# Cached attention on one core: V in products of N 512, kept K in pairs of N 256, shorter chain bursts, and wo in runs of 1792 B

## The chip, the core and the metric

The kernel runs on one core of a Trainium2 chip. The metric is the device time of one execution in microseconds (us), and a kernel's number is the median of its runs. Executions of one kernel on one chip spread by about 0.4% either way here (1114.97 to 1125.07 us in one set of the changed kernel), so a difference of 3 us or less between two kernels is mostly not resolved. All timed runs quoted below were in the fast state, except the single run of experiment 10, whose state can't be told.

## The reference, cut to what matters

Two passes, each of attention over a cache and of a small MLP block, for eight batch rows with one query token each. There are 16 query heads on 8 K/V heads of width 256, and 4096 cached keys. Everything is bf16, and D is 448.

```python
x = x + _A_ref(_layernorm(x), A_k_cache, A_v_cache, A_wq, A_wo)   # attention
x = x + _B_ref(_layernorm(x), B_w1, B_w2, B_w3, B_w4)             # MLP block
x = x + _A_ref(_layernorm(x), A_k_cache, A_v_cache, A_wq, A_wo)   # the same caches again
x = x + _B_ref(_layernorm(x), B_w1, B_w2, B_w3, B_w4)

# _A_ref: scores = q k^T / 16, p = softmax(scores), o = p v, then o.reshape(B, 1, 4096) @ wo
```

K and V are 134 MB each. Pass 2 of a row needs the result of pass 1 of that row, and the same K and V again. What the kernel can't keep in SBUF in between it has to read twice.

## The kernel before

K and V come in chunks of 1 MB. SBUF has 15 "places" of one chunk each. While a batch row goes from its first pass to its second, 11 of its chunks stay in their places (the kept ones), and so only 4 places are left for everything else to stream through. A place is given back when its chunk has been used, and the next load into it is issued at once:

```python
NC = 15
kept = [(GP - 1, kv, n) for n in range(4) for kv in range(2)] + [(GP - 2, 0, n) for n in range(3)]
slots = [consts.tile([128, 16 * Dh], BF16, name=f"slot{n}") for n in range(NC)]
...
for idx, it in enumerate(items):            # one item = one chunk of K (kv 0) or V (kv 1)
    ...
    if kv == 0:
        transpose_k(slot)                   # two DVE stream transposes, 1.2 us each
        step(idx)                           # the chain may put one burst here
        scores(slot, c, st["q"], gp)        # 32 products, N 128
        if c == 0 and n - 1 in p_of:
            transpose_p(p_of.pop(n - 1))    # p of the task before: 4 products and an ACT cast
        ...
    else:
        step(idx)                           # and here
        pv(st["o", g8], slot, c, gp, begin=...)   # 16 products, N 256
        ...
    if not (ps == 0 and stays(it)):
        places.append(p)
    emit_loads()                            # loads into the places that are free
    step(idx)                               # and here
```

The "chain" is what turns one row's o into the q of its second pass: normalisation, wo, layer norms, the MLP and wq. It is a Python generator. Each `yield` ends one burst of it, and `step` places the next burst between the chunks, in the program order of the engines:

```python
def add_cols(y_ps, rhs, w, rows, every, open=None):
    for fc in range(5):
        ...
        for i in rows:
            nc.tensor.matmul(r, w[:, i, lo:hi], rhs(i), ...)
        ...                                 # a yield after every `every` columns fc

def half(o_ps, zall, g8, OT):               # evacuation of o: twice per row and pass
    rz = yield from z_cols(zall, range(2 * g8, 2 * g8 + 2))
    R = chn.tile([128, 8], FP32, tag="R")
    ...
    nc.scalar.copy(o_sb[:], o_ps[:, 0:Dh])
    in_use.remove(o_ps)
    yield
    for j in range(2):
        nc.tensor.matmul(ot_ps[:, j], o_sb[:, 128 * j : 128 * j + 128], R[:], start=True, stop=True)
    yield
    nc.vector.tensor_copy(OT[:, :, 8 * g8 : 8 * g8 + 8], ot_ps)
    yield
```

Each engine's instructions stand in one program order, and the dip shown below has them run in it: a V product waits there behind a burst of the chain although its data has landed. A burst that stands ahead of the scores or of V can delay these, with them the moment at which the place is free, and with that the next load.

The softmax here doesn't subtract the row's maximum and nothing guards it: scores larger than these inputs give would overflow.

Of the kernel before, what the change touches and what calls it, by code (L numbers as in the profile page):

```python
# [8 lines left out]
FP32 = mybir.dt.float32  # L9
# [8 lines left out]
def kernel(  # L18
# [52 lines left out]

    slots = [consts.tile([128, 16 * Dh], BF16, name=f"slot{n}") for n in range(NC)]

# [21 lines left out]
    for u in range(2):  # L95
# [6 lines left out]

    fold = consts.tile([128, 8], FP32, name="fold")
    nc.vector.tensor_reduce(
        fold[:],
        ident.rearrange("p (q n) -> p n q", q=4)[:, 0:8],
        mybir.AxisListType.X,
# [169 lines left out]
    def project_q(b0, nb, qT):  # L277

        yield from norm(xT[:, :, b0 : b0 + nb], nb, False)
        q_ps = room_ps("q", nb).rearrange("p (c b) -> p c b", b=nb)  # L280
        for j in range(2):
            for h in range(Hq):
                for fc in range(4):
                    w, xi = wblk(wq_sb, HD, 2 * h + j, fc)
                    nc.tensor.matmul(  # L285
                        q_ps[:, j * Hq + h, :],
                        w,
                        xbs(nb)[:, xi, :],
                        start=(fc == 0),
                        stop=(fc == 3),  # L290
                    )
                if h % 8 == 7:
                    yield
        nc.vector.tensor_copy(qT, q_ps)
        yield
# [54 lines left out]
    def mlp_hidden(b0, nb):  # L350
# [3 lines left out]
        for c in range(HC):  # L354
            for fc in range(4):
                w, xi = wblk(w3_sb, F, c, fc)
                nc.tensor.matmul(  # L357
                    h_ps[:, c * nb : c * nb + nb],
                    w,
                    xbs(nb)[:, xi, :],  # L360
                    start=(fc == 0),
                    stop=(fc == 3),
                )
            if c == HC // 2:
                yield
# [25 lines left out]
    def mlp(b0, nb):  # L391
        HT = yield from mlp_hidden(b0, nb)
        yield from out_cols(lambda c: HT[:, c, :], w4_sb, HC, b0, nb, 2)

# [31 lines left out]
    def half(o_ps, zall, g8, OT):  # L426


        rz = yield from z_cols(zall, range(2 * g8, 2 * g8 + 2))

        R = chn.tile([128, 8], FP32, tag="R")
        nc.vector.tensor_mul(
            R[:].rearrange("p (g n) -> p g n", n=4),
            rz[:].rearrange("p n g -> p g n"),
            fold[:].rearrange("p (g n) -> p g n", n=4),
        )
        o_sb = chn.tile([128, Dh], FP32, tag="o_sb")
        nc.scalar.copy(o_sb[:], o_ps[:, 0:Dh])  # L438
        in_use.remove(o_ps)
        yield  # L440
        ot_ps = ot_bank[:, 32 * g8 : 32 * g8 + 16].rearrange("p (j h) -> p j h", j=2)
        for j in range(2):
            nc.tensor.matmul(  # L443
                ot_ps[:, j], o_sb[:, 128 * j : 128 * j + 128], R[:], start=True, stop=True
            )
        yield
        nc.vector.tensor_copy(OT[:, :, 8 * g8 : 8 * g8 + 8], ot_ps)
        yield
# [3 lines left out]
    def first_half(b, st):  # L452

        OT = work.tile([128, 2, Hq, 1], BF16, tag="OT", bufs=1)
        st["OT"] = OT
        yield from half(st["o", 0], st["z"], 0, OT[:, :, :, 0])
        yield from add_cols(
            y_room(1)[:, 0], lambda i: OT[:, i % 2, i // 2], wo_sb, range(NB2 // 2), 2
        )

    def chain(b, st):
        OT = st["OT"]
        yield from half(st["o", 1], st["z"], 1, OT[:, :, :, 0])
        yield from add_cols(
            y_room(1)[:, 1], lambda i: OT[:, i % 2, i // 2], wo_sb, range(NB2 // 2, NB2), 2
        )
# [90 lines left out]
    where = {}  # L557

    def emit_loads(most=None):
        n = 0  # L560
        while loads and places and n != most:
            it = loads.pop(0)
            p = where[it] = places.pop(0)
            if stays(it):
# [20 lines left out]

    def scores(t, x, qbd, gp):
        kv = t[:].rearrange("p (k t e i r) -> p k e r t i", k=4, t=4, e=4, r=2)
        for n in range(8):
            half, e2, par = n // 4, (n // 2) % 2, n % 2
            ep = 4 * e2 + 2 * par + half  # L590
            for k in range(4):
                nc.tensor.matmul(  # L592
                    sc[32 * k : 32 * k + 8, 128 * x : 128 * x + 128],
                    qbd[:, ep, gp].rearrange("p a h -> p (a h)"),
                    kv[:, k, 2 * half + e2, par],
                    start=(n == 0),
                    stop=(n == 7),
                )
# [41 lines left out]
    def pv(o_ps, v, a, gp, begin):  # L640


        g = 2 * gp + a // 2
        for y in range(16):
            q = y % 4
            at = 128 * a + 8 * (4 * q + y // 4) + 6 - 2 * (g % 4)
            nc.tensor.matmul(  # L647
                o_ps[32 * q : 32 * q + 8, 0:256],
                ptz[:, at : at + 8],
                v[:, y * Dh : (y + 1) * Dh],  # L650
                start=(begin and y < 4),
                stop=(y >= 12),
                skip_group_check=True,
            )

    def pv_cols(o_ps, v, a, gp):

        g = 2 * gp + a // 2
        for y in range(16):
            for j in range(2):  # L660
                nc.tensor.matmul(  # L661
                    o_ps[:, j, 2 * g : 2 * g + 2],
                    v[:, y * Dh + 128 * j : y * Dh + 128 * j + 128],
                    ptw[:, a, 4 * (y % 4) + y // 4, 6:8],
# [12 lines left out]
    emit_loads(5)  # L677
    nc.sync.dma_start(wo_sb[:], A_wo.rearrange("(g p) d -> p g d", p=128))
    load_split(w3_sb, B_w3, F)
# [16 lines left out]
    def step(idx):  # L696

        for kind in ("chain", "last", "rest"):
# [5 lines left out]
            if e["n"] < e["of"] * (idx - e["at"] + 1) / max(e["until"] - e["at"], 1):  # L704
                e["n"] += 1
                if next(e["g"], gens) is gens:
                    gens.remove(e)

    first_of = {}
    for idx, (n, kv, c) in enumerate(items):  # L710
# [3 lines left out]
    for idx, it in enumerate(items):  # L714
        n, kv, c = it
        ps, b, gp = tasks[n]
        if (ps, b, gp, kv, c) == (0, Bn - 1, REST, 0, 0):
            assert pairs_done[1, MID - 1] == 4
            add_gen("rest", 0, rest(), idx + 1, idx + 18, 21)
        p = where[(b, gp), (kv, c)] if ps == 1 and (stays(it) or inside(it)) else where[it]  # L720
        slot = slots[p]
        final = (ps, b) == (1, Bn - 1)
        if kv == 0:
# [19 lines left out]
            step(idx)  # L743
            scores(slot, c, st["q"], gp)
            if c == 0 and n - 1 in p_of:
                transpose_p(p_of.pop(n - 1))
            if c == 1:
# [7 lines left out]
        else:  # L755
# [34 lines left out]
            if c == 3:  # L790
                done = pairs_done[ps, b] = pairs_done.get((ps, b), 0) + 1
                if done == 2 and ps == 0:
                    add_gen("chain", b, first_half(b, st), idx + 1, idx + 21, 9)
                elif done == 2:
                    add_gen("chain" if final else "last", b, first_last(b, st), idx + 1, idx + 13, 9)
                elif done == 4 and ps == 0:
                    add_gen("chain", b, chain(b, st), idx + 1, first_of[(1, b), 0] - 1, 30)
                elif done == 4 and not final:
                    add_gen("last", b, last(b, st), idx + 1, idx + (7 if b == Bn - 2 else 13), 6)
        if not (ps == 0 and stays(it)):  # L800
# [78 lines left out]
```

## Time and profile before

| | before |
|---|---|
| time, median (lowest to highest) | 1128.83 us (1124.52 to 1134.04), 6 runs |
| span of the profiled execution | 1124.9 us |
| TensorE busy | 63% |
| bytes moved by the core's queue | 446.80 MB |
| lack against 420 GB/s, worked out from the row of GB/s: first two slices / middle / last slice | 7.8 / 30.9 / 16.6 us |

The last row is the way in which this document counts. The page has 40 equal slices with the GB/s of each. What a slice lacks to 420, times the length of a slice, divided by 420, is the time for which the stream stood still; slices above 420 count as no lack. The same sum is used for every kernel below.

The groups of instructions that the change touches, from the kernel before's page. The columns are line, engine (PE is TensorE, DVE is VectorE, ACT is ScalarE), operation, output<-input, shapes and count, then total busy us and mean ns of one, then the engine's idle us just before them with what ended most of it:

```profile
L592 PE MATMUL sc<-slot,qbd 128*8 128x128 bf16 x8192 | 277.3, 292 | 297.0 <-DVE slot L584 241.5
L647 PE MATMUL o<-slot,ptw 128*8 128x256 bf16 x3968 | 248.1, 398 | 58.4 <-DMA slot<-in_A_v_cache_dram 39.6
L443 PE MATMUL misc<-R,o_sb 128*128 128x8 f32 x124 | 30.4, 356 | 1.1 <-ACT o_sb L438 1.1
```

The first is the scores, the second V, the third the products of the evacuation. The scores wait for the DVE transposes of K, and V waits for its DMA: TensorE is not what they lack.

How a burst of the chain costs stream time is seen in a dip, from the timeline of the kernel before (start us, length us, engine, line, what, in brackets the idle time before it and what ended it; SPq is the queue that issues loads):

```profile
141.91 2.19 PE L339 MATMUL misc<-OT,wo_sb 128*128 128x1 bf16 x48
...
144.03 1.03 PE L647 MATMUL o<-slot,ptw 128*8 128x256 bf16 x16
144.14 0.16 DVE L468 TENSOR_TENSOR xT<-xT,misc 128x4 f32<-128x4 f32 x1 [2.81 <-PE misc L339]
...
145.00 2.36 DVE L584 STREAM_TRANSPOSE slot<-slot 128x1024 uint32<-128x1024 uint32 x2
145.10 0.33 SPq L576 DMA_DIRECT2D slot<-in_A_v_cache_dram  x1
...
148.06 0.33 SPq L576 DMA_DIRECT2D slot<-in_A_k_cache_dram  x1
```

By the semaphores of their loads, a V chunk had landed at 141.18 and a K chunk at 143.67. V waits on TensorE until the 48 products are through. Its place goes to the next load at 145.10, 3.91 us after the landing; a V chunk that nothing holds up takes 1.11 us (landed at 425.83). K waits on VectorE: the chain's additions and norms stand ahead of its transposes, and the first of them waited 2.81 us for the same burst. So the transposes start at 145.00, and the place goes at 148.06, 4.39 us after the landing instead of the usual 3.09. Not every burst costs this. The one at 387.33 that the prediction shows is as long, but it ran while the transposes of the next K did (from 387.42), and that K place was given back at 390.52, 3.10 us after they began. For the K before it that was 3.07 us (382.47 to 385.54).

The Trainium skill, "Perfetto Trace Analysis", Optimization Strategy, describes the pattern: the same gap, repeating for a stretch on what should be saturated, "can mean there isn't enough SBUF/PSUM for the next tile to be allocated". The trace agrees: the dips lie in the stretches with 4 free places, and a load that finds a place early, in a good stretch, takes 20 us from issue to landing, and one in a dip 7.8 us. That a further place would close the dips is not shown: the run that tried it (experiment 12) failed.

### The profile page before, as it was taken

The numbers are of one execution on the slowest core, as the hardware profiler recorded it, in microseconds if no ns is written. First come the engines' busy times: TensorE is split into PE (matmuls) and PEld (weight loads), VectorE is DVE, ScalarE is ACT, GpSimd is POOL, SyncE is SP. The second block draws the span as 40 slices with busy tenths as digits, with TensorE's granted clock in tenths as the row PEclk, the third lists the DMA queues.
The fourth block names the chain that finished last, engine by engine and source line by source line (L and its number), as shares of the span: only waits on it lengthen the run. The fifth ranks groups of instructions, "written<-read, shape, count | busy, mean of one in ns | idle before, by whom it ended". The sixth has DMA issues, their size and how long they took to land. (4 is left out here: it accounts for less than half of the span.)

```text
span 1124.9 us, 36977 instructions
## 1 busy us (share of the span) xinstructions
PE 707.0 (63%) x17173; PEld 518.8 (46%) x17173; DVE 590.0 (52%) x1009; ACT 123.9 (11%) x362; POOL 15.6 (1%) x25
## 2 busy tenths in 40 slices
PE   3145577556754577645784477745778477877776
PEld 2123456435642455424563255523556255655555
DVE  5145464646365555555465453655537553575462
ACT  0001001110110011100011001100111001111010
POOL 0000000000000000000000000000000000000000
PEclk9999999655575555555556555655555555565575
DMA  9999999999999999999999999999999999999994
GB/s 352 371 420 420 413 372 419 419 411 397 403 419 420 387 385 419 417 420 387 401 420 419 420 387 415 419 420 407 389 401 419 419 394 400 419 381 397 405 419 172
DMA packets 67241, 449.15 MB, mean 399 GB/s; under 512 B 6920, under 2 KB 12944, under 8 KB 13456
## 3 DMA queue, kind: packets, MB, share of 16 engines
q1 hardware_dynamic: 67056, 446.80, 98.0%
q8 instruction: 134, 2.20, 0.8%
q14 instruction: 19, 0.16, 0.0%
q10 hardware_dynamic: 32, 0.00, 0.0%
HBM read 446.77 MB, written 0.01 MB: 397 GB/s over the span
## 5 line engine op out<-in xcount | busy, mean ns | idle before, releaser
L584 DVE STREAM_TRANSPOSE slot<-slot 128x1024 uint32<-128x1024 uint32 x400 | 469.1, 1218 | 270.8 <-DMA slot<-in_A_k_cache_dram 270.5
L592 PE MATMUL sc<-slot,qbd 128*8 128x128 bf16 x8192 | 277.3, 292 | 297.0 <-DVE slot L584 241.5
L592 PEld LDWEIGHTS <-qbd 128*8 128x8 bf16 x8192 | 195.0, 108 | 374.3 <-issue 191.6
L647 PE MATMUL o<-slot,ptw 128*8 128x256 bf16 x3968 | 248.1, 398 | 58.4 <-DMA slot<-in_A_v_cache_dram 39.6
L601 ACT ACTIVATE p_n<-sc 128x256 bf16<-128x256 f32 x128 | 95.3, 745 | 769.9 <-PE sc L592 769.9
L647 PEld LDWEIGHTS <-ptw 128*8 128x8 bf16 x3968 | 111.8, 112 | 105.7 <-issue 54.3
L339 PEld LDWEIGHTS <-wo_sb 128*128 128x128 bf16 (+1 forms) x1600 | 62.6, 122 | 21.4 <-issue 20.8
L339 PE MATMUL misc<-OT,wo_sb 128*128 128x1 bf16 (+1 forms) x1280 | 53.5, 176 | 7.3 <-issue 5.2
L285 PEld LDWEIGHTS <-wq_sb 128*128 128x128 bf16 x1152 | 34.9, 104 | 24.6 <-issue 18.8
L311 DVE TENSOR_SCALAR qbd<-misc,quad 128x64 bf16<-128x64 f32 x64 | 13.7, 277 | 59.8 <-PE misc L305 59.8
L635 ACT CAST ptw<-misc 128x128 bf16<-128x128 f32 x64 | 17.4, 272 | 196.8 <-PE misc L628 105.6
L285 PE MATMUL misc<-xb,wq_sb 128*128 128x1 bf16 x1024 | 32.3, 166 | 7.9 <-DVE xb L260 4.4
L601 ACT ACTIVATION_READ_ACCUMULATOR p_n<-sc 128x1 f32 x128 | 34.0, 266 | 0.0
L443 PEld LDWEIGHTS misc<-R,o_sb 128*128 128x128 f32 x124 | 27.6, 310 | 10.2 <-issue 8.0
L443 PE MATMUL misc<-R,o_sb 128*128 128x8 f32 x124 | 30.4, 356 | 1.1 <-ACT o_sb L438 1.1
L243 POOL TENSOR_TENSOR t<-t,nhalf 128x2 f32<-128x2 f32 (+2 forms) x18 | 13.3, 739 | 1095.7 <-DVE t L250 1095.7
L339 PEld LDWEIGHTS <-w_sb 128*128 128x128 bf16 (+1 forms) x630 | 25.1, 125 | 7.3 <-issue 7.1
L357 PE MATMUL misc<-xb,w_sb 128*128 128x1 bf16 (+1 forms) x560 | 17.9, 166 | 12.4 <-DVE xb L260 7.4
L357 PEld LDWEIGHTS <-w_sb 128*128 128x128 bf16 x560 | 17.7, 105 | 17.0 <-issue 16.9
L412 PE MATMUL misc<-zm,one 128*128 128x8 f32 (+1 forms) x66 | 18.6, 352 | 9.8 <-ACT ptw L635 6.5
L619 DVE STREAM_TRANSPOSE slot<-store 128x512 uint32<-128x512 uint32 x32 | 20.1, 684 | 7.2 <-PE sc L592 7.2
L339 PE MATMUL misc<-HT_t,w_sb 128*128 128x1 bf16 (+1 forms) x560 | 22.8, 177 | 1.5 <-issue 1.2
(94 smaller groups left out, 239.5 us busy)
## 6 DMA issues: line engine op xcount, KB each, us to landing
slot<-in_A_v_cache_dram SPq DMA_DIRECT2D x216, 1024.0 KB, 11.6
slot<-in_A_k_cache_dram SPq DMA_DIRECT2D x200, 1024.0 KB, 12.1
wo_sb<-in_A_wo_dram SPq DMA_DIRECT2D x1, 3584.0 KB, 26.8
wq_sb<-in_A_wq_dram SPq DMA_DIRECT2D x3, 1024.0 KB, 7.0
w_sb<-in_B_w_dram SPq DMA_DIRECT2D x1, 1568.0 KB, 12.8
w_sb<-in_B_w_dram SPq DMA_DIRECT2D x3, 448.0 KB, 26.8
wq_sb<-in_A_wq_dram SPq DMA_DIRECT2D x2, 256.0 KB, 10.0
w_sb<-in_B_w_dram SPq DMA_DIRECT2D x2, 112.0 KB
```

The lines of the kernel that those rows point to most:

```text
L285: nc.tensor.matmul(q_ps[:, j * Hq + h, :], w, xbs(nb)[:, xi, :], start=(fc == 0), stop=(fc == 3),)
L311: nc.vector.tensor_scalar_mul(qbd[:, :, :, a, :], qs.rearrange("p e (f g u h) -> p (e f) u g h", f=2, u=2, h=2)[:, :, u], quad[:, a : a + 1],)
L339: nc.tensor.matmul(r, w[:, i, lo:hi], rhs(i), start=start, stop=stop, skip_group_check=open is not None,)
L357: nc.tensor.matmul(h_ps[:, c * nb : c * nb + nb], w, xbs(nb)[:, xi, :], start=(fc == 0), stop=(fc == 3),)
L412: nc.tensor.matmul(z_ps, ones, zm[:], start=True, stop=True)
L443: nc.tensor.matmul(ot_ps[:, j], o_sb[:, 128 * j : 128 * j + 128], R[:], start=True, stop=True)
L584: nc.vector.transpose(w, w)
L592: nc.tensor.matmul(sc[32 * k : 32 * k + 8, 128 * x : 128 * x + 128], qbd[:, ep, gp].rearrange("p a h -> p (a h)"), kv[:, k, 2 * half + e2, ...
L601: nc.scalar.activation(p_sb[:, :, :, 2 * u : 2 * u + 2].rearrange("p t i x -> p x t i"), sc[:, 256 * u : 256 * u + 256].rearrange("p (x t ...
L619: nc.vector.transpose(slot[:].bitcast(U32)[:, 512 * n : 512 * n + 512], store[n][:].bitcast(U32))
L635: nc.scalar.copy(ptw[:, :, :, 6:8], pt_ps.rearrange("p t k (a h) -> p a (t k) h", a=4),)
L647: nc.tensor.matmul(o_ps[32 * q : 32 * q + 8, 0:256], ptz[:, at : at + 8], v[:, y * Dh : (y + 1) * Dh], start=(begin and y < 4), stop=(y >= ...
```

## The change

The intent: fewer TensorE instructions for V and for kept K, no long bursts of the chain in front of the places' release, less work between a K chunk's landing and its release, and wo in longer DMA runs.

V takes two 256-wide blocks of a chunk per product (N of 512). The two land beside each other in o, with weights of 16 columns, so that o has two diagonal parts, and the evacuation needs two copies and twice the products:

```diff
-        for y in range(16):
-            q = y % 4
-            at = 128 * a + 8 * (4 * q + y // 4) + 6 - 2 * (g % 4)
-            nc.tensor.matmul(
-                o_ps[32 * q : 32 * q + 8, 0:256], ptz[:, at : at + 8],
-                v[:, y * Dh : (y + 1) * Dh], ...
+        rows = v[:].rearrange("p (i q d) -> p q i d", q=4, d=Dh)
+        for i in (0, 2):
+            for q in range(4):
+                at = 128 * a + 8 * (4 * q + i) + 6 - 2 * (g % 4)
+                nc.tensor.matmul(
+                    o_ps[32 * q : 32 * q + 16, :].rearrange("p (i d) -> p i d", i=2),
+                    ptz[:, at : at + 16], rows[:, q, i : i + 2], ...
...
-        nc.scalar.copy(o_sb[:], o_ps[:, 0:Dh])
+        for n in range(2):
+            nc.scalar.copy(o_sb[:], o_ps[:, Dh * n : Dh * n + Dh])
+            yield
+            for j in range(2):
+                nc.tensor.matmul(ot_ps[:, n, j], o_sb[:].rearrange("p (i j) -> p j i", j=2)[:, j], R[:, n], ...)
...
+        nc.vector.tensor_copy(half_o[:], ot_ps[:, 0])
+        nc.vector.tensor_add(to, half_o[:], ot_ps[:, 1])
```

The places become one tensor, loads choose neighbouring places for a pair of kept K chunks, and the pair is scored with one product of N 256 where they are neighbours. The transposition of p moves between the two halves of the scores:

```diff
-            scores(slot, c, st["q"], gp)
-            if c == 0 and n - 1 in p_of:
-                transpose_p(p_of.pop(n - 1))
+            turn = None
+            if c == TURN(n) and n - 1 in p_of:
+                turn = lambda t=p_of.pop(n - 1): transpose_p(t)
+            if not paired(n, c):
+                scores(p, c, st["q"], gp, between=turn)
+            elif c % 2 != ps:
+                ...
+                if abs(two[1] - two[0]) == 1:
+                    scores(two[0], x, st["q"], gp, also=two[1], between=turn)
```

The chain is cut into smaller bursts, and has more steps to be placed:

```diff
-                if h % 8 == 7:                 # wq
+                if h % 4 == 3:
-            if c == HC // 2:                   # w3
+            if c % 4 == 3:
-        yield from out_cols(lambda c: HT[:, c, :], w4_sb, HC, b0, nb, 2)
+        yield from out_cols(lambda c: HT[:, c, :], w4_sb, HC, b0, nb, 1)
-            y_room(1)[:, 0], ..., wo_sb, range(NB2 // 2), 2
+            y_room(1)[:, 0], ..., wo_sb, range(NB2 // 2), 1
-                    add_gen("chain", b, chain(b, st), idx + 1, first_of[(1, b), 0] - 1, 30)
+                    add_gen("chain", b, chain(b, st), idx + 1, first_of[(1, b), 0] - 1, 43)
```

Two neighbouring rows of wo lie on one partition, so that a run is 1792 B instead of 896 B. The last V chunks and the evacuation therefore take their weights with a column step of 2:

```diff
-    nc.sync.dma_start(wo_sb[:], A_wo.rearrange("(g p) d -> p g d", p=128))
+    nc.sync.dma_start(
+        wo_sb[:].rearrange("p (h j) d -> p h (j d)", j=2),
+        A_wo.rearrange("(h p j) d -> p h (j d)", p=128, j=2),
+    )
-                    v[:, y * Dh + 128 * j : y * Dh + 128 * j + 128],
+                    v[:, y * Dh + j : (y + 1) * Dh : 2],
```

## The prediction

> **What bounds the kernel now.** I read the head of the page first, then its row of GB/s, then the DMA issues and the engine shares of single stretches, and last the timeline of one slow stretch. Page, rows of the whole span and of its 40 slices:
>
> ```profile
> span 1124.9 us, 36977 instructions
> PE 707.0 (63%) x17173; PEld 518.8 (46%) x17173; DVE 590.0 (52%) x1009; ACT 123.9 (11%) x362; POOL 15.6 (1%) x25
> ...
> PEclk9999999655575555555556555655555555565575
> ...
> GB/s 352 371 420 420 413 372 419 419 411 397 403 419 420 387 385 419 417 420 387 401 420 419 420 387 415 419 420 407 389 401 419 419 394 400 419 381 397 405 419 172
> ```
>
> No compute engine is above 63%, while half of the slices move 417 to 420 GB/s, which is evidently what this stream can reach: 446.8 MB at 420 would need 1064 us. The kernel is a transfer with holes in it. A slice is 28.12 us; adding up what each lacks to 420 gives 826, and 826 x 28.12 / 420 = 55.3 us. Of it the first two slices hold 7.8 us (start, small packets), the last 16.6 us (work after the last transfer), and the rest 30.9 us, in eight dips that come every 100 to 135 us. What the change can win is in those 30.9 us and a little at the ends.
>
> What a dip is: stretches of 14.06 us (columns: length, busy of PE, PEld, DVE, ACT, POOL with counts, clock, DMA share, GB/s), two without a dip and three of one:
>
> ```profile
> 337.44:351.50 14.06, 6.54 (x148) 3.79 (x148) 8.78 (x10) 1.03 (x3) 0.00 (x0) 0.50 1.01 421
> 351.50:365.56 14.06, 6.34 (x148) 3.88 (x148) 7.11 (x6) 1.57 (x5) 0.00 (x0) 0.50 1.01 421
> 379.62:393.68 14.06, 10.85 (x224) 8.26 (x220) 6.78 (x16) 1.29 (x4) 0.00 (x0) 0.50 0.94 355
> 393.68:407.74 14.06, 9.10 (x232) 6.64 (x231) 9.18 (x21) 1.43 (x5) 0.70 (x1) 0.50 0.98 375
> 407.74:421.80 14.06, 11.41 (x259) 8.62 (x257) 6.72 (x17) 1.77 (x6) 0.55 (x1) 0.50 0.99 394
> ```
>
> The dips are where the "chain" (wo, norms, MLP, wq of one batch row) runs. They coincide with the phase in which 11 of the 15 places of SBUF hold kept chunks, so only 4 are left to stream through. The DMA issues of a dip (380 to 425 us) and of a good stretch (450 to 500 us), last column issue to landing:
>
> ```profile
> slot<-in_A_v_cache_dram SPq DMA_DIRECT2D x10, 1024.0 KB, 7.8
> slot<-in_A_k_cache_dram SPq DMA_DIRECT2D x8, 1024.0 KB, 7.9
> ...
> slot<-in_A_k_cache_dram SPq DMA_DIRECT2D x9, 1024.0 KB, 20.5
> slot<-in_A_v_cache_dram SPq DMA_DIRECT2D x8, 1024.0 KB, 20.2
> ```
>
> A landing of 20 us means eight transfers queued, 7.8 us two to three: in a dip the queue is short, because places come back late. A pair (one K and one V chunk) takes 5.0 us at 420 GB/s; the K transposes of this dip start at 377.79, 382.47, 387.42, 393.52, 398.47, 404.41, 409.46 and 415.21, that is 5.35 us apart. What PE and DVE do to a pair there, from the timeline:
>
> ```profile
> 377.79 2.36 DVE L584 STREAM_TRANSPOSE slot<-slot 128x1024 uint32<-128x1024 uint32 x2
> 379.08 0.60 PE L592 MATMUL sc<-slot,qbd 128*8 128x128 bf16 x16 [2.18 <-DVE slot L584]
> 380.20 0.60 PE L592 MATMUL sc<-slot,qbd 128*8 128x128 bf16 x16 [0.53 <-DVE zs_t L401]
> 381.95 1.02 PE L647 MATMUL o<-slot,ptw 128*8 128x256 bf16 x16
> 382.90 1.02 PE L443 MATMUL misc<-R,o_sb 128*128 128x8 f32 x4
> 387.33 2.19 PE L339 MATMUL misc<-OT,wo_sb 128*128 128x1 bf16 x48
> ```
>
> **What the Trainium skill says.** (1) "TensorE: Matmul & The Clock Gate", section Back-to-back issue gap: on the throttled clock products follow each other by N / 1.2 ns, so by columns streamed, not by instructions. The trace agrees: in the V burst at 381.95 the four column groups start within 12 ns of each other and the next four 213 ns later (256 / 1.2), and the clock column is 0.50 in nearly all slices after the first 200 us. The earlier 9s are not to be believed: score bursts there have the same 0.60 us. (2) The same page, Weight-path perf modes: fast weight load takes full 128-column weights with a column step other than 1. No record of the kernel before has such a step, so the trace is silent. (3) "DMA: Bandwidth & Descriptors", Why small descriptors are slow: a fixed cost per packet. The trace agrees: packets of 896 B take 47 ns, of 3584 B 145, of 8192 B 309.
>
> **The change part by part.**
>
> V in products of N 512: 3968 products become 1984. Columns streamed per group stay 4 x 256 = 2 x 512 = 1024, 853 ns at half clock. Only issue falls away, and it was not the limit, so a burst should stay about 1.0 us. Value in the dips: about 0.
>
> Kept K in pairs of N 256: reading the changed program, 56 pairs occur, and 35 lie in neighbouring places and so merge; 35 x 32 = 1120 products fewer of 8192. Again the same columns. And kept chunks are scored while filling or draining the places, where the DMA row stands at 419 to 421, not in the dips. Value 0. Choosing neighbours holds a load back 21 times, by one or two chunks, with 13 to 15 chunks still ahead: no cost. The order of the 416 loads is the same in both programs.
>
> The price: o now has two diagonal parts, so each of the 31 evacuations makes two ACT copies (0.38 us more), doubles the L443 products (1.02 us more PE) and adds a DVE operation (0.17). PE in all 31 x 1.02 = 32 us, but per dip of some ten pairs about two evacuations: +2 us per ten pairs, +0.2 us per pair if PE were always the limit; it is idle a quarter of the dip, so I take +0.1.
>
> Smaller bursts: the chain goes from 29 to 40 steps in the same 19 items. I counted: it now uses both step points of every item and ends two items later, still in time. The sum of chain work stays; the longest burst falls from 2.19 us (48 products) to about 0.5 at a time. What is won is that V no longer waits behind a long burst: I estimate 0.15 us per pair.
>
> Transpose of p between the score halves: 0.29 us of PE and the ACT cast after it now fall into the 0.53 us in which PE waits for DVE. Per task of four pairs about 0.5 us, 0.12 per pair.
>
> Sum per pair: 0.1 - 0.15 - 0.12 = -0.17 of the excess of 0.35. Scaled to 30.9 us, and discounted by half since part of it only moves the wait to DVE or to DMA latency: -8 us.
>
> wo in runs of 1792 B: 3.67 MB came at 338 GB/s, so 10.9 us. The packet times above lie on a line, which puts 1792 B at 80 ns; estimate 370 GB/s, so 9.9 us: -1 us, straight off the stream.
>
> The end: the last V chunks go through 128-column weights now taken at step 2. If loads stay fast, 0; else up to +5 us.
>
> Total: 1129.4 - 8 - 1 = 1120 us.
>
> **The rivals.** (a) The merged products free PE and the dips close: all 30.9 us back, 1098 us. For it: PE is at 11 of 14 us there. Against: columns, not instructions, set the bursts. (b) The dip is set by the loop landing, 2.36 us of DVE transposes, scores, reissue, with 4 places; PE bursts hide under it and nothing moves: 1127 to 1129. For it: K scores wait for DVE in nearly every pair. (c) The doubled evacuation lands in the dips at full price: 0.2 x 10 pairs x 8 dips = +16 us less what the bursts win, 1130 to 1135. (d) Strided weights load slowly and the end grows: +5 us on any of these.
>
> **Range and chances.** I put most weight between (b) and my sum, some on half of (a). Range 1106 to 1130. Faster by 2% means below 1106.8, which needs 22.6 of about 32 us that can be had: 0.10. Slower by 2% means above 1152; (c) with (d) does not reach it: 0.02. Within 2%: 0.88.
>
> **What would show it.** The V burst in the dips still 1.0 us (x8); the score group near 277 us busy less little; clock still 0.5; L443 twice the count and near 60 us. The eight dips still there but shallower, near 390 to 400 GB/s, with lost time some 23 us in place of 30.9; landings in a dip a little above 8 us; slices two steps in a little above 371. No burst of the chain over about 1 us. I am wrong if V bursts shrink clearly (issue was the limit), if dips vanish, or if the last slice loses far more than 16.6 us (strided weights).

## The result, and the profile after

| | before | after |
|---|---|---|
| time, median (lowest to highest), 6 runs each | 1128.83 us (1124.52 to 1134.04) | 1120.98 us (1117.90 to 1122.72) |
| ratio after / before, with its 95% interval | | 0.9929 (0.9901 to 0.9957) |
| lack against 420 GB/s: first two slices / middle / last slice | 7.8 / 30.9 / 16.6 us | 6.5 / 24.8 / 16.9 us |

A ratio is the mean time of one kernel's fast runs over that of the other's of the same rounds, so it is not quite the ratio of the medians. A second set of six runs (the first experiment) gave 0.9901, so the change is worth 8 to 11 us.

The head of the changed kernel's page:

```profile
span 1116.1 us, 31093 instructions
...
PE 727.6 (65%) x14193; PEld 454.4 (41%) x14193; DVE 595.6 (53%) x1040; ACT 136.1 (12%) x393; POOL 15.6 (1%) x25
...
PEclk9995556655565557555575555655556555565565
...
GB/s 357 385 421 421 415 393 420 420 401 420 417 419 421 401 411 420 420 422 388 410 419 421 417 398 403 419 421 397 388 385 421 417 402 401 419 372 408 409 418 166
```

TensorE has 2980 products fewer and is busier, 727.6 us for 707.0. The good slices still stand at 417 to 422, the dips are all there, and most of them are shallower (the one in slices 28 to 30 is deeper: 397, 388 and 385 for 407, 389 and 401). The time is in the middle: 30.9 - 24.8 = 6.1 us, and 1.3 us at the start.

The groups that answer to those of before, from the page:

```profile
L660 PE MATMUL sc<-places,qbd 128*8 128x128 bf16 (+1 forms) x7072 | 267.8, 306 | 252.6 <-DVE places L645 215.1
L716 PE MATMUL o<-places,ptw 128*16 128x512 bf16 x1984 | 241.0, 583 | 75.4 <-DMA places<-in_A_v_cache_dram 72.8
L447 PE MATMUL misc<-R,o_sb 128*128 128x8 f32 x248 | 60.6, 355 | 10.7 <-ACT o_sb L442 5.0
```

V has half the products and only 7 us less of busy time in all (and a chunk's burst stays as long, below): the columns count, not the instructions. The evacuation has doubled, to 60.6 us.

The dip that the prediction shows, from 379.62 on, in the changed kernel (length, busy of PE, PEld, DVE, ACT, POOL with counts, clock, DMA share, GB/s):

```profile
379.62:393.68 14.06, 10.27 (x214) 6.64 (x218) 9.24 (x22) 1.29 (x5) 0.70 (x1) 0.50 1.00 390
393.68:407.74 14.06, 11.57 (x209) 8.01 (x201) 7.55 (x17) 1.59 (x5) 0.00 (x0) 0.50 1.01 417
407.74:421.80 14.06, 10.90 (x222) 6.34 (x222) 3.11 (x14) 1.01 (x3) 0.55 (x1) 0.50 1.00 411
```

355, 375 and 394 GB/s have become 390, 417 and 411, with TensorE as busy as before and at the same half clock. The stretch ahead of it, from 365.56 on, moved 409 for 417: the dip begins earlier and is shallower. What a burst looks like there, from the changed kernel's timeline:

```profile
376.67 1.02 PE L447 MATMUL misc<-R,o_sb 128*128 128x8 f32 x4 [0.52 <-ACT o_sb L442]
...
379.54 1.03 PE L716 MATMUL o<-places,ptw 128*16 128x512 bf16 x8
...
383.98 1.68 PE L341 MATMUL misc<-OT,wo_sb 128*64 128x1 bf16 x32
...
392.94 0.29 PE L696 MATMUL misc<-identb,p_n 128*128 128x32 bf16 x4
...
393.53 0.60 PE L660 MATMUL sc<-places,qbd 128*8 128x128 bf16 x16 [0.30 <-DVE zs_t L403]
```

A V burst of 8 products takes 1.03 us, as the 16 of before did. The evacuation's burst is as long as before and comes twice. The longest burst of the chain here is 1.68 us, for 2.19. Where a burst meets the evacuation it is still more: 28 products of w4 and the evacuation's 4 follow each other at 401.33 and 402.62 and take 2.31 us, and this comes five times. What fell is the number of long stretches. Between 100 and 1060 us TensorE works for over 1.5 us on neither scores nor V 30 times in the kernel before and 15 times here, 17 in the second profile (products that follow within 150 ns counted as one stretch). The transposition of p (392.94) now lies where TensorE waited for DVE between the two halves of the scores: the second half starts after 0.30 us of idle time where it usually has 0.53.

The weights that are now read with a column step of 2, in the last V chunks, from the groups by shape of the kernel before (first) and of the changed kernel (second):

```profile
L661 PEld LDWEIGHTS <-slot 128*128 128x128 bf16 x256 | 7.8, 105 | 2.2 <-issue 2.1
```

```profile
L730 PEld LDWEIGHTS <-places 128*128 128x128 bf16 x256 | 8.1, 106 | 1.1 <-issue 0.6 <-DMA places<-in_A_v_cache_dram 0.5
```

105 and 106 ns each: the step costs nothing.

### The profile page after: what moved, and what is told of

It is laid out like the page before. It is cut to its first block, busy times and chain, and to the rows that moved or that the text cites. A ratio compares the mean times of both kernels' runs of the same rounds, so it can differ in the third digit from the quotient of the medians.

```text
span 1116.1 us, 31093 instructions
## 1 busy us (share of the span) xinstructions
PE 727.6 (65%) x14193; PEld 454.4 (41%) x14193; DVE 595.6 (53%) x1040; ACT 136.1 (12%) x393; POOL 15.6 (1%) x25
## 4 chain that ended last, share of the span: by engine, by line
DMA 62%; PE 18%; DVE 13%; SPq 3%; issue 2%; ACT 1%; POOL 0%; POOLq 0%; DVEq 0%; ACTq 0%
DMA places<-in_A_k_cache_dram 53%; DVE places L645 10%; DMA places<-in_A_v_cache_dram 9%; PE sc L660 8%; PE o L716 4%; PE misc L341 3%; PE misc L447 2%; SPq L161 2%; SPq L637 1%; DMA wq_sb<-in_A_wq_dram 1%; DVE qbd L313 1%; PE misc L287 0%; ACT p_n L669 0%; POOL t L245 0%; DVE places L687 0%
## 5 line engine op out<-in xcount | busy, mean ns | idle before, releaser
L645 DVE STREAM_TRANSPOSE places<-places 128x1024 uint32<-128x1024 uint32 x400 | 469.0, 1218 | 259.8 <-DMA places<-in_A_k_cache_dram 258.9
L660 PE MATMUL sc<-places,qbd 128*8 128x128 bf16 (+1 forms) x7072 | 267.8, 306 | 252.6 <-DVE places L645 215.1
L660 PEld LDWEIGHTS <-qbd 128*8 128x8 bf16 x7072 | 167.5, 106 | 356.6 <-issue 180.3
L716 PE MATMUL o<-places,ptw 128*16 128x512 bf16 x1984 | 241.0, 583 | 75.4 <-DMA places<-in_A_v_cache_dram 72.8
L716 PEld LDWEIGHTS <-ptw 128*16 128x16 bf16 x1984 | 44.5, 102 | 91.2 <-issue 82.3
L447 PEld LDWEIGHTS misc<-R,o_sb 128*128 128x128 f32 x248 | 55.3, 309 | 30.8 <-issue 20.1
L447 PE MATMUL misc<-R,o_sb 128*128 128x8 f32 x248 | 60.6, 355 | 10.7 <-ACT o_sb L442 5.0
L287 PE MATMUL misc<-xb,wq_sb 128*128 128x1 bf16 x1024 | 34.6, 166 | 9.3 <-DVE xb L262 6.0
L442 ACT COPY o_sb<-o 128x256 f32<-128x256 f32 x62 | 23.5, 379 | 71.5 <-PE misc L447 63.3
L687 DVE STREAM_TRANSPOSE places<-store 128x512 uint32<-128x512 uint32 x32 | 20.1, 684 | 11.2 <-PE sc L660 11.2
```

The source lines that it names most:

```text
L287: nc.tensor.matmul(q_ps[:, j * Hq + h, :], w, xbs(nb)[:, xi, :], start=(fc == 0), stop=(fc == 3),)
L442: nc.scalar.copy(o_sb[:], o_ps[:, Dh * n : Dh * n + Dh])
L447: nc.tensor.matmul(ot_ps[:, n, j], o_sb[:].rearrange("p (i j) -> p j i", j=2)[:, j], R[:, n], start=True, stop=True,)
L645: nc.vector.transpose(w, w)
L660: nc.tensor.matmul(sc[32 * k : 32 * k + 8, 128 * x : 128 * (x + nx)], qbd[:, ep, gp].rearrange("p a h -> p (a h)"), v, start=(n == 0), sto ...
L687: nc.vector.transpose(slot[:].bitcast(U32)[:, 512 * n : 512 * n + 512], store[n][:].bitcast(U32))
```

## The experiments

The theory after the result: the stream loses time where a place is given back late, and the change wins because no long burst of the chain stands in front of the release. The rivals: the bigger products (V, pairs) win it, or the moved transposition of p does, and the doubled evacuation gives part of it back.

Twelve experiments ran. The first four shared one chip and 19 runs of the kernel before (1129.88 us); experiments 5, 6, 7 and 8 shared another (30 runs, 1130.71); 9, 10 and 11 a third (14 runs, 1131.76); 12 a fourth (7 runs, 1133.29). Between calls I compare ratios to the kernel before, within a call medians too. The diffs are against the changed kernel.

**1. The changed kernel again.** No edit.

> The changed kernel again, as the measure for the three that follow on the same chip. Ratio to before near 0.993, the time lost in the eight dips near 25 us against 31 in the kernel before (to 420.5 GB/s). If dips differ by more than 3 us in sum from the first profile (24.8), single profiles can't tell parts of 2 us apart.

Measured: 1119.43 us (1114.97 to 1125.07, 6 runs), ratio 0.9901 (0.9872 to 0.9929). In its profile the middle lacks 20.3 us, for 24.8 in the first profile of the very same kernel. A single profile's sum of holes therefore moves by some 4 us from one execution to the next, and differences of that size between single profiles are not read below.

**2. V in products of N 256, with the single evacuation.**

```diff
-        for n in range(2):
-            nc.scalar.copy(o_sb[:], o_ps[:, Dh * n : Dh * n + Dh])
+        nc.scalar.copy(o_sb[:], o_ps[:, 0:Dh])
...
-        for i in (0, 2):
-            for q in range(4):
-                nc.tensor.matmul(o_ps[32 * q : 32 * q + 16, :]..., rows[:, q, i : i + 2], ...)
+        for y in range(16):
+            nc.tensor.matmul(o_ps[32 * q : 32 * q + 8, 0:256], ptz[:, at : at + 8], v[:, y * Dh : (y + 1) * Dh], ...)
```

> The changed kernel with V in products of N 256 again, and so with one evacuation of o in place of two; all else stays. My theory (columns, not instructions, set the V burst; the second evacuation only costs): 0.1 us a pair better, some 2 to 5 us less than the changed kernel, ratio to before 0.989 to 0.992. Rival (fewer, longer products are what won): the win goes, ratio 0.997 to 1.0.

Measured: 1118.08 us (1114.06 to 1126.85, 6 runs), ratio 0.9900 (0.9867 to 0.9932). It is 1.35 us below experiment 1, far inside the intervals. The bigger products of V and the second evacuation that they require together neither win nor cost anything that can be seen. The run does not separate the two; that the products alone save nothing is read from the V burst, 1.03 us for 1.02.

**3. The chain in bursts as before.**

```diff
-                if h % 4 == 3:
+                if h % 8 == 7:
-            if c % 4 == 3:
+            if c == HC // 2:
-        yield from out_cols(lambda c: HT[:, c, :], w4_sb, HC, b0, nb, 1)
+        yield from out_cols(lambda c: HT[:, c, :], w4_sb, HC, b0, nb, 2)
-            ... wo_sb, range(NB2 // 2), 1
+            ... wo_sb, range(NB2 // 2), 2
```

(and the totals of steps: 10 for 14, 31 for 43, 21 for 25)

> The changed kernel with the chain in the large bursts of before (32 to 48 products), all else stays. My theory (V waits behind bursts, 0.15 us a pair): 5 to 7 us slower than the changed kernel, ratio 0.997 to 1.0, dips near 30 us. Rival (the loop of landing, transposes and scores sets the dips, bursts lie under it): no difference, ratio 0.992 to 0.994.

Measured: 1126.22 us (1122.96 to 1129.97, 14 runs), ratio 0.9970 (0.9956 to 0.9984). That is 6.8 us above experiment 1, and the two intervals of the ratio don't meet. (Against the changed kernel's first set, 0.9929, it would be 4.6 us, and the intervals just overlap.) Most of the change's gain is in the size of the bursts. Its timeline and its row of GB/s show the old picture again:

```profile
384.03 2.38 PE L341 MATMUL misc<-OT,wo_sb 128*128 128x1 bf16 x64
```

```profile
GB/s 356 383 420 421 415 395 398 420 409 395 389 421 420 405 384 409 419 421 408 383 417 420 421 400 379 420 421 411 394 393 420 421 408 401 420 402 413 390 418 172
```

The middle lacks 29.7 us, nearly what it lacked before (30.9), while the start keeps its gain (6.7).

**4. The transposition of p after the scores, as before.**

```diff
-            if c == TURN(n) and n - 1 in p_of:
-                turn = lambda t=p_of.pop(n - 1): transpose_p(t)
...
+            if c == 0 and n - 1 in p_of:
+                transpose_p(p_of.pop(n - 1))
```

> The changed kernel with the transpose of p after the scores again and not between their halves, all else stays. My theory (0.12 us a pair): 4 to 5 us slower than the changed kernel, ratio 0.996 to 0.998. Rival: no difference, since V waits for its transfer or for DVE anyway.

Measured: 1122.11 us (1118.84 to 1124.37, 6 runs), ratio 0.9926 (0.9903 to 0.9949). That is 2.7 us above experiment 1, with intervals that overlap: the direction is as predicted, and the size is not resolved. What the move does on TensorE is plain in the V group, by shape, of this experiment:

```profile
L716 PE MATMUL o<-places,ptw 128*16 128x512 bf16 x1984 | 239.7, 581 | 83.7 <-DMA places<-in_A_v_cache_dram 75.3 <-ACT ptw L703 6.7 <-ACT o_sb L442 1.5
```

In the changed kernel V's wait for the ACT cast of p (ptw) is 0.8 us in all. Here it is 6.7. So 5.9 us of waiting of V are removed by the move, over the whole kernel, and only part of that can become stream time.

**5. Each product of the evacuation twice.** The second writes the same values again, so the result stays right.

```diff
-            for j in range(2):
+            for j in (0, 1, 0, 1):
```

> The changed kernel with every product of the evacuation of o issued twice (same result), 31 x 2 x 1.02 = 63 us more on PE in short bursts of 2 us, some 16 to 20 of them within the dips. It doubles the suspected cost of the second evacuation. If PE work in the dips counts in full: 15 us or more over the changed kernel, ratio above 1.002. If only long holds count: some 4 to 8 us, ratio 0.993 to 0.998, with the places held over 3.5 us rising from 12 toward 25. If PE has room: no difference, 0.988 to 0.992.

Measured: 1136.91 us (1135.10 to 1139.04, 4 runs), ratio 1.0065 (1.0041 to 1.0088), slower than the kernel before. By the ratios it is (1.0065 - 0.9901) x 1130 = 18.5 us slower than the changed kernel in experiment 1, and 15.4 us slower than in its first set (0.9929). From its page and its timeline:

```profile
L447 PE MATMUL misc<-R,o_sb 128*128 128x8 f32 x496 | 109.0, 348 | 10.5 <-ACT o_sb L442 5.0
```

```profile
382.77 1.88 PE L447 MATMUL misc<-R,o_sb 128*128 128x8 f32 x8 [0.52 <-ACT o_sb L442]
```

TensorE got 109.0 - 60.6 = 48.4 us more work, in bursts of 1.88 us instead of 1.02, and 15 to 18.5 of it came through. In experiment 2 the opposite step, from 60.6 us of evacuation to 30.3, gave 1.35 us. The evacuation's TensorE work is thus neither free nor charged at a fixed rate. I read it so that a burst of 1.02 us still fits into most waits and one of 1.88 us does not, as with the chain's bursts in experiments 3 and 6. No run separates the length of these bursts from their sum. Nor is the second evacuation always hidden: in the changed kernel four of the five V chunks that are released late (the count is explained below) have 2.02 us of other products between landing and start, the last burst of w4 and the second burst of the evacuation (landed at 403.98, released at 407.78).

**6. The chain in bigger bursts than before.**

```diff
-                if h % 4 == 3:
+                if h == Hq - 1:
-            if c % 4 == 3:
-                yield
-            ... wo_sb, range(NB2 // 2), 1     # and w4
+            ... wo_sb, range(NB2 // 2), 5
```

> The changed kernel with the chain in bursts larger than before: all 80 products of a half of wo, all 56 of w3, all 70 of w4, 64 of wq at a time. Same PE work. If the length of a burst makes the dips: clearly slower than the kernel before, ratio 1.003 to 1.012, places held over 3.5 us above 30. If the large bursts mattered for another reason (the number of steps), no more than with the bursts of before: 0.997.

Measured: 1135.11 us (1133.18 to 1140.10, 7 runs), ratio 1.0061 (1.0038 to 1.0083). By the ratios it is 15 to 18 us slower than the changed kernel (its two sets), with the same products in the same total and only grouped otherwise. From its timeline:

```profile
391.10 3.04 PE L341 MATMUL misc<-OT,wo_sb 128*128 128x1 bf16 x80
...
394.07 1.30 PE L714 MATMUL o<-places,ptw 128*16 128x512 bf16 x8
...
395.40 0.33 SPq L635 DMA_DIRECT2D places<-in_A_v_cache_dram  x1
```

A single burst of 3.04 us holds back V, landed at 390.57, and the release of its place until 395.40. The middle lacks 41.3 us. Burst size moves the time in both directions from the kernel before, without a change in the amount of work. With the size the number of steps changes too (43, 31 and 23 for the changed kernel, experiment 3 and this one), so these two are not told apart.

**7. V at N 256 and no pairs: bursts, moved transposition and wo alone.** The edit of experiment 2, and `return False` at the head of `paired`.

> The changed kernel without both of its named parts: V in products of N 256 with one evacuation, K chunks never paired. Left are the smaller bursts, the transpose of p between the halves, and wo in runs of 1792 B. If my theory holds it wins as much as the whole: ratio 0.988 to 0.992. If the longer products carry part of the win: 0.995 or more.

Measured: 1121.32 us (1118.94 to 1124.70, 6 runs), ratio 0.9928 (0.9907 to 0.9949). The first set of the whole change had 0.9929. The second had 0.9901, and the intervals overlap. The bigger products can be left out of the change, and the gain, as far as it is resolved, stays.

**8. V at N 256, and a chain step between the two halves of the scores too.** The idea was to fill the 0.53 us in which TensorE waits there.

```diff
-                scores(p, c, st["q"], gp, between=turn)
+                scores(p, c, st["q"], gp, between=turn or (lambda: step(idx)))
```

> The run with V at N 256 and a third place for a step of the chain in each K chunk that is scored alone: between the two halves of its scores, where PE waits 0.53 us for DVE in the profile before. If bursts ahead of V and K are what holds places, this is faster than the changed kernel by 2 to 5 us, ratio 0.985 to 0.989; if what is left is the loop itself, no difference, 0.989 to 0.991; if the burst overruns the wait and delays the second half, slower.

Measured: 1134.53 us (1129.58 to 1136.60, 22 runs), ratio 1.0032 (1.0021 to 1.0044), slower than the kernel before and a miss. A chain burst there took 0.56 to 0.58 us in the dip at 380 to 395 us, a little more than the 0.53 us that it was meant to fill, and can itself wait for VectorE first (0.59 us at 382.11). It stands straight ahead of the second half of the scores, hence of the release of the K place. The median time from a K chunk's landing to the next load into its place rose from 3.09 to about 3.7 us, and the middle lacks 37.7 us.

**9. No pairs.** `return False` at the head of `paired`.

> The changed kernel with kept K chunks never paired; V stays in products of N 512. My theory (pairs are outside the dips and save no columns): no difference to the changed kernel, ratio 0.989 to 0.994. Rival (the run without both parts came out 3 us slower than the one without the longer V alone, so pairs win something): 0.994 to 0.997.

Measured: 1122.46 us (1118.34 to 1127.74, 9 runs), ratio 0.9926 (0.9902 to 0.9951). Not told apart from the changed kernel (0.9901 and 0.9929 in its two sets).

**10. wo in runs of 896 B as before**, with contiguous weights in the last chunks and in the evacuation.

```diff
-        wo_sb[:].rearrange("p (h j) d -> p h (j d)", j=2),
-        A_wo.rearrange("(h p j) d -> p h (j d)", p=128, j=2),
+        wo_sb[:],
+        A_wo.rearrange("(g p) d -> p g d", p=128),
-                    v[:, y * Dh + j : (y + 1) * Dh : 2],
+                    v[:, y * Dh + 128 * j : y * Dh + 128 * j + 128],
```

> The changed kernel with wo loaded in runs of 896 B again (and its d split in halves again). One profile: the time lost in the first 60 us goes back from 6.65 to about 8.0 us, packets of 896 B at 47 ns; the rest of the trace alike. The single time says nothing at this size.

Measured: one look, 1121.46 us, which by itself says nothing. The transfer does. The DMA issues of the page (bytes, and us from issue to landing) for this experiment, then for the changed kernel:

```profile
wo_sb<-in_A_wo_dram SPq DMA_DIRECT2D x1, 3584.0 KB, 26.8
```

```profile
wo_sb<-in_A_wo_dram SPq DMA_DIRECT2D x1, 3584.0 KB, 25.5
```

The kernel before has 26.8 too. The second slice of the row of GB/s, in which wo lands, is 371 before and 370 here, and 380 to 385 in every kernel with the longer runs. The lack in the first two slices goes back to 7.8 us, where the changed kernel has 6.5. The packets themselves, in the trace: 47 ns for 896 B, and 78 ns for 1792 B.

**11. V at N 256, and the chain's steps moved:** none in front of V, and up to three after it, when its place has been given back.

```diff
         else:
-            step(idx)
             ...
-        step(idx)
+        for _ in range(3 if kv else 0):
+            step(idx)
```

> The run with V at N 256 and the steps of the chain moved: none between the scores of a K chunk and the V product after it, up to three after V, ahead of the next K. If V held behind the chain is what is left of the dips, the V hold falls from 2.2 us on average toward 1.5 and the time by 3 to 8 us, ratio 0.983 to 0.988. If the steps in a row then wait for each other on DVE and delay K instead: K holds rise above 3.2 us, ratio 0.992 or more.

Measured: 1119.28 us (1114.59 to 1120.11, 6 runs), ratio 0.9895 (0.9867 to 0.9923). Neither branch came: the mean time from V's landing to the next load into its place fell as intended, from 2.18 us in experiment 2 to 1.63, but the time is not told apart from the changed kernel's. The holds of K over 3.5 us rose at the same time (from 4 in experiment 2 to 12). The work that no longer stands ahead of V stands ahead of the next K. By the count used above, this run has 31 stretches of over 1.5 us, as many as experiment 3 (31) and twice those of the changed kernel, without being slower than the latter. So the length of a burst alone does not decide: it matters what the burst stands in front of.

**12. One more place to stream through:** ten kept chunks instead of eleven.

```diff
-    kept = [... for kv in range(2)] + [(GP - 2, 0, n) for n in range(3)]
+    kept = [... for kv in range(2)] + [(GP - 2, 0, n) for n in range(2)]
```

> The changed kernel keeping 10 chunks of a batch row in place of 11, so that five places are left to stream through and 8.4 MB more are read, 20.0 us more at 420 GB/s. If the dips are the loop of four places (landing, hold, reissue), a fifth closes them: time lost between 60 us and the end of the stream below 8 us against 21 to 25, time about 1120 + 20 - 15 = 1125, ratio 0.994 to 0.999, GB/s of every inner slice above 410. If the dips come from the chain competing for the memory or for the DMA itself, they stay: ratio 1.005 to 1.012.

Measured: 1154.40 us (1152.48 to 1154.89, 4 runs), ratio 1.0194 (1.0154 to 1.0234). The edit was faulty, and its time says nothing about a fifth place. In pass 1 all K chunks of that head group are scored as pairs when the second of the pair is reached. The third chunk was no longer kept, so its place had been given back and loaded again by then. The product of the pair waits for that new load and reads wrong keys (the comparison with the reference still passed, so its tolerance does not see it). The wait is in the timeline:

```profile
367.38 1.88 PE L660 MATMUL sc<-places,qbd 128*8 128x256 bf16 x32 [28.89 <-DMA places<-in_A_v_cache_dram]
```

There is one such hole per row. It was the last run, so what a fifth place would do stays open.

**What the late releases have in common.** From each trace I took, for every chunk that streams through after the first 120 us, the time from its landing to the issue of the next load into its place (its "hold"), and counted those over 3.5 us. About a seventh of the chunks can't be matched and are left out. Chunks that land long before their turn, with a full queue, are not meant either: these are held up to 20 us without harm. A recount, with the places taken from the kernels' own assignment and only chunks that landed within 12 us of issue and were held under 7.4 us, gives 26 for the kernel before, 10 and 11 for the changed kernel and 33, 49, 36 and 41 for experiments 3, 6, 5 and 8. It differs from the table by up to six, in the same order but for near equals.

| kernel | holds over 3.5 us: K + V | mean hold of V, us | middle lack, us | median, us |
|---|---|---|---|---|
| 2. V 256 | 4 + 3 | 2.18 | 21.5 | 1118.1 |
| 1. changed kernel, second profile | 6 + 6 | 2.35 | 20.3 | 1119.4 |
| 11. steps moved | 12 + 1 | 1.63 | 26.3 | 1119.3 |
| 7. bursts, transposition, wo alone | 3 + 2 | 2.16 | 30.2 | 1121.3 |
| changed kernel, first profile | 6 + 5 | 2.32 | 24.8 | 1121.0 |
| 10. wo as before | 6 + 6 | 2.32 | 26.8 | 1121.5, one run |
| 9. no pairs | 5 + 5 | 2.31 | 25.3 | 1122.5 |
| 4. transposition as before | 16 + 6 | 2.50 | 29.7 | 1122.1 |
| 3. old bursts | 14 + 17 | 2.55 | 29.7 | 1126.2 |
| before | 10 + 13 | 2.38 | 30.9 | 1128.8 |
| 6. big bursts | 15 + 28 | 2.97 | 41.3 | 1135.1 |
| 8. step between halves | 36 + 6 | 2.29 | 37.7 | 1134.5 |
| 5. evacuation doubled | 20 + 13 | 2.65 | 40.1 | 1136.9 |

The kernels with few long holds (5 to 13) take 1118 to 1122.5 us, those with 31 to 43 take 1126 to 1137. Two rows fit badly: experiment 4 has as many as the kernel before (22 and 23) in 7 us less, and experiment 7 has the fewest but a large lack. Both were profiled in a run at the slow end of their own range (1124.2 and 1124.7 us). The mean hold says less: the changed kernel's V hold is 2.32 us for 2.38 before, and in experiment 11 it fell to 1.63 for nothing. I read from this that the tail costs: with four places, a single late one leaves the queue short, and a hold that is shorter than usual does not make up for it. But it is a correlation, found after the runs, and no run changes the tail alone.

The late K chunks are mostly held up on VectorE, not by products ahead of their scores. In nine of the ten of the kernel before, the transposes began 0.7 to 1.3 us after the landing, behind instructions of the chain on VectorE, and from their end to the next load it took the usual 0.7 us. So a chain that waits on TensorE also blocks the K transposes that follow it in VectorE's program order. No run tests this path alone.

No experiment beat the changed kernel beyond the noise. Experiments 2 and 11 have lower medians (1118.08 and 1119.28 us), which are not told apart from its 1119.43.

## Why the prediction was right

The median of 1120.98 us lies 1 us from the predicted 1120, and the class, within 2%, was the likeliest. A hit this close is partly luck: two sets of the same kernel differ by more (1120.98 and 1119.43), and two errors below cancel. The points, by the prediction's own steps:

- **The bound: right.** The kernel is a transfer with holes. The good slices stand at 417 to 422 before and after, TensorE gained 20.6 us of busy time, and the kernel still became faster. The dips lost 24.8 us (20.3 in the second profile) where about 23 was announced.
- **V at N 512, value 0: right.** The burst stayed at 1.03 us, and experiment 2 took the big products away without a loss. Rival (a), the dips close because the merged products free TensorE, is refuted by this and by experiment 7. (In the lines behind this step, the V burst at 381.95, the second and third step between groups of four are 213 ns, but the first is 169 ns.)
- **Pairs, value 0: right within the noise.** Experiment 9 can't be told apart from the changed kernel; a value of 1 or 2 us would not be seen.
- **Smaller bursts: right in mechanism and size.** The 0.15 us per pair of an excess of 0.35 are 13.2 of the 30.9 us, and halved by the discount 6.6 us. Experiment 3 measured 6.8, or 4.6 against the first set. Experiment 6 moved the same lever the other way, to 1135.11 us. The announced limit on the burst was missed: the longest of the chain in the dip is 1.68 us, not "about 1" (32 products, of which the last have 64-column weights), and 2.31 us with the evacuation behind it. "V no longer waits behind a long burst" holds for the long holds, from 13 to 5, and not for V on average. The prediction left out that the bursts also hold up the transposes of K, through VectorE.
- **Transposition of p: the direction fits, the size was too large.** Its 0.12 us per pair come to 5.3 us with the discount. Experiment 4 measured 2.7, not resolved from 0. The wait of V for p that it removes is 5.9 us in all by the trace, so 5.3 was nearly all of it, and too much to expect from the stream.
- **The second evacuation: too high as a price.** Its +0.1 us per pair come to 4.4 us. Experiment 2 bounds what it and the bigger products do together near 1.35 us, not resolved. These two errors, 2.6 us too much gain and some 3 us too much cost, cancelled in the sum. (The three parts come to 0.17 / 0.35 x 30.9 / 2 = 7.5 us, which the prediction wrote as 8.) Rival (c), the evacuation at full price, does not hold for the change as it is. It does come true when the evacuation is doubled once more (experiment 5: 15 to 18.5 of 48.4 us). The price is not linear in TensorE time.
- **wo, -1 us: right.** The landing came 1.3 us earlier, the first two slices lack 1.3 us less, and a packet took 78 ns for the predicted 80.
- **The end, 0 or up to +5: it was 0.** The weights with step 2 load in 106 ns for 105, and the last slice lacks 16.9 us for 16.6. Rival (d) is out.
- **Rival (b), the loop of landing and transposes sets the dips and nothing moves:** refuted as a whole by experiments 3 and 6, where the bursts alone move the time by 6.8 and by 15 to 18 us. It may well set the floor that remains: the 20 to 25 us of holes in the middle that none of the parts closed. That was not shown.

Open: the parts of 1 to 3 us each (pairs, V's products and the second evacuation, transposition) are below what these runs resolve. So is whether a fifth place closes the remaining dips.

## What to carry to other kernels

When a stream runs through few buffers, look at what stands in program order ahead of the release of a buffer, on every engine that the release passes through, and cut that into short pieces or move it to where the engine would wait anyway. Here the number of long bursts ahead of a release went with the time: regrouping the same products moved it by 5 to 18 us (experiments 3 and 6), while 2980 products fewer won nothing that could be seen. Merging products into wider ones won nothing here, where the columns streamed stay the same. Before you fill a wait with other work, compare the piece's length with the wait, and ask what the piece itself waits for: a filler that overruns it lands on the critical path.

## What the Trainium skill lacked or had wrong

- "TensorE: Matmul & The Clock Gate", Weight-path perf modes, allows fast weight load with a column step from -1,023 to 1,024 elements but gives no time for a step other than 1. Here 256 loads of 128 bf16 columns took 106 ns each at step 2, and 105 ns at step 1.
- "DMA: Bandwidth & Descriptors", Why small descriptors are slow, gives the fixed part of a packet as about 3 cycles, and 32 B of metadata. Packets here took 47, 78, 145 and 309 ns for 896, 1792, 3584 and 8192 B. That is a line of 0.0356 ns per byte (from the last two) with 14 to 17 ns of fixed time, which the page's figure doesn't let a reader foresee.
- The same page, Where 436 GB/s comes from, says that for transfers from HBM to SBUF the HBM side of about 358 GB/s binds. For this program on one core that is too low: about half of the slices moved 417 to 422 GB/s. Another section of the page marks its own 425 GB/s as single-core.
- None has it: how late the release of a buffer may be before the stream notices. Here, with four free places of 1 MB, the four kernels with over 30 holds above 3.5 us took 1126 to 1137 us, and those with 13 or fewer 1118 to 1122.5. Two with 22 and 23 took 1122 and 1129, so this is a correlation and no threshold.
